# Inverse-spectra scratch by blocks of 128 rows, last transform in 128x32 tiles, and another order of operations in an H3 long convolution plus gated GLU with all gradients

## The chip, the cores and the metric

The kernel runs on one core of one Trainium2 chip. The metric is device microseconds of one execution, where less is better; the time of a kernel is the median of its runs. One further execution was recorded by the hardware profiler, and every line of a profile shown here comes from such a recording.

The engines go by these names: PE is TensorE (matmuls; PEld is the loading of their weights), DVE is VectorE, ACT is ScalarE, POOL is GpSimd, and SP is SyncE, which in this kernel issues every DMA (its queue is SPq). Data lies in a 2-dimensional on-chip memory of 128 partitions (here one array, `big`); matmul results land in PSUM (one array, `PP`).

## The reference, cut to what matters

The input is one sequence of S = 2048 rows and D = 512 channels in bf16. The function is a residual sum of a long convolution branch and a gated GLU branch over a normalised input; the kernel computes its value and the gradients of nine inputs for a given output gradient.

```python
xn = _layernorm(x)                       # x = A_q
# branch A: short shift convolution of k, times v, long convolution, times q
k_shift = sum over t of k_pad[:, t:t + S, :] * shift_k[:, ks - 1 - t]     # ks = 4
kv = k_shift * v
y = irfft(rfft(kv, 2 * S) * rfft(ssm_k, 2 * S))[:S] + kv * ssm_D
A = xn * y
# branch B, F = 1376
B = ((xn @ w_gate) * (xn @ w_up)) @ w_down
out = x + A + B
# and the vector-Jacobian product of out for A_q, A_k, A_v, shift_k, ssm_k, ssm_D, w_gate, w_up, w_down
```

The long convolution of length 4096 is done by matmuls with tables of sines and cosines, in two stages each way. Three spectra come back through the inverse transform: the convolution's value (in the code signal 0, `py[0]`), the gradient of kv (signal 1) and the gradient of ssm_k (signal 2). A row of the scratch that carries them between the two stages of the inverse therefore has 3 x 512 = 1536 elements, 3072 bytes.

## The kernel before

**Recording and order.** The body of the kernel runs no instruction itself. Every call goes through a small class `Eng`, which appends it to a list of operations; consecutive matmuls into the same PSUM slot, and the matmuls between `together()` and `apart()`, become one operation (a TensorE group). At the end `emit(PLAN)` unpacks a string: the order in which all operations are emitted, and the PSUM bank of every slot. The order of instructions on each engine, SyncE's DMA queue included, is the order of that list; nothing else decides it. Since all instructions are emitted by one line of `Eng`, every line of the profile says L173, and operations are told apart by tile names and shapes.

**Stages.** (1) The GLU's forward and data-gradient rows by strips j of F (0 to 5), with the strips' h, dg and du stored to a DRAM scratch `HD`; alongside it layernorm, and `dw_gen(j)`, the weight gradients of a strip, which end in stores of 1 MB and less to `ow`. (2) `a_gen`: first stage of the forward transforms, stored to the scratch `AX` in 16 stores of 768 KB. (3) `s_gen`, over i = 0 to 7: `s_B(i)` second stage forward, `s_pw` the pointwise products of spectra on VectorE, `s_Bi(i)` first stage inverse (L542). Each `s_Bi(i)` is three groups of 16 matmuls; ScalarE copies each result to one of two buffers `sp["C"][s]`, and four stores (L549) put them into the scratch `CX`, one of 384 KB for each s and g. (4) The rest goes by chunks n = 0 to 7 of 256 sequence rows:

- `c_load(n)` (L651 to L658) loads 1.5 MB of CX into `f["C"]`, of which there is only one: c_load(n+1) may start when the last transform of chunk n has read it. For n = 0 it is four loads, each to every fourth partition; three of them need no store of i = 7.
- `last_dft(n)` (L695 to L702) is the second stage of the inverse: 12 matmuls of 64 output rows, two side by side in the array.
- `c_dkv`, `c_y` and `c_o5` (L731 to L736) copy the three signals out of PSUM, multiply them by v, k_shift, xn and the output gradient, and store the results of v's and ssm_k's gradients (`o3`, `o5`; the first row of the latter also goes to `o6`, ssm_D's gradient).
- `c_dsk(n)` forms products for shift_k's gradient on VectorE and sums them over partitions by eight matmuls of 32 output rows (a P sum); `dk_pair` is k's gradient, on VectorE.
- `hd_load(n)` (L619) is a transposing DMA of the strips' rows from HD into one of two buffers; `y_o` and `y_x` are the block products with the weights (11 and 22 matmuls of 128x512 for each half chunk) that need it, and their results end in stores of `o0` and `o1`.

Each `hd_load` stands in SyncE's one queue with everything else. The order in that queue around the end of stage 3 is: weight-gradient store, the four stores of i = 7, hd_load(0), the last quarter of c_load(0), c_load(1). The buffers of the chunks lie partly over those of earlier stages in `big`: hd_load(1) overwrites the buffer from which the last weight-gradient store of strip 5 reads.

The scratch CX is declared with 8 chunks, each padded by 2048 elements (4 KB):

```python
CX = dram.tile([8, 512 * 3 * D + 2048], BF, name="CX")[:, 0:512 * 3 * D]
```

Of the kernel before, what the change touches and what calls it, by code (L numbers as in the profile page):

```python
# [10 lines left out]
BF = mybir.dt.bfloat16  # L11
# [6 lines left out]
S = 2048  # L18
D = 512
F = 1376  # L20
R = 16
# [6 lines left out]
NCH = 8  # L28
# [1 line left out]
RING = 28  # L30
RO = [0, 16, 24, 40, 56, 72]
EPS = 1e-5
PLAN = "c-lP|1FSC1uI&_au5H`4ZQHhO+qP}nwr$%s-*@hxyv)wFskUu4MPxt#hyu|e21J5%kRCEa2FM7RAPZ!LT#ya2LvF|ec_AM-U=UC+@DKzcAS8r>&=3Z~LO2Ky?H~f=fTR!;qC!Nd1;rp5#D=&K3(7+rC<^f)KBR>N;3Wklgk+E(DnLOf06C!$)P{;s2?|4TC;_FQG8BO-Pz|a=V`u{1p(*r$p3n?>!Dy%s?V&W(ff`T~2Ekw`3B92nG>7`o0s25c=nG?@E_8(c&;rInD;Nj!pe4+Q6>tPPL2GCL3!pO$fPpX`y1+u101e?WOocWu5hg(y=n7?F8nlI@Fdb&XZWscyU=eJD#jq5Xz$VxXTi_E+hD$IEX22d83M*j>#KjA+4A#IZh==iUD-4HiFdKHjcGw9Ca4jr{UGN!3z<$^ZA0ZK>hQyEx(!d<}1tVcK9DsfB1-`;TSO<q-J)D4(a14&aDL4(^AS5QlM3@-UVG=wC=`krL!{m4kZox&k4CmoG+<+_a9j?M{xCuYtCxpV3kOY#$ANT+j@gdxY6qpiI;RARAk03Rs!L;}cLSq<=h)*FbhQsg}0asxL%!rvVGiJf8$XE%pVP&j>*|93-z?_&1b7M8kgL$z!8Y&9r!@F<?&ca{Vh=hQMjj#qb#wOSlo8eGwjxDeyK8IE~3|~NNY=dpFCPv1n7zJx#ZES~iurAia_Baw>!zefm<={80#MQV4*Wx-{k8@!IguqC+AERLq=0}I!U^%L6LXV@cJ`TqYI09cn1MG;e;0?Tkw{QR(;%FR$8?XRQ#7Q_7$Kf;_j}ve@&cK=22@B#ZEQGVMFc!hixEZ(LHtd33u^V>B9@rCm;XGV`i?BBq#Xi^<n^8Y3hW&8>4#Yut5a;4#+>3{B3LeHII3E|{VqAhtaVt*6=va%kV{;meF>nPI#}ZhVVqt8oPbIMh)uuW4ga%SQiit;Y5DlgwG?b3xFgk_}s3p~*M%0joQxj@R?WqHu#8Oxq%V1e7hvo4EPN&m2gU;Y7Y)j{`0=A>ecm=OwREkE?DF(%)Yj_=F(G9$bx9~RJ!Mk`5@8bh}h_UGr#-X_M7@y!%e1`GpIljP`_zGX+8+?oJ@I8LOj~JigV1GJ~7jY(Cz*#h#E>bI+Lp$&je#S5O6~Ezk{DD957yiaS_!ohYh#Vy#CZU9sh!T^Mk*B#dg630ex<r?09$lfUv>S)u0BQt{={=mqeRu{g;Z({_L6n1XQZC9(A*dJa#9i2%_TYIMMR_PBC8Ok&f>Kf_3Qegf427j|l$Y{RcuGxaC@qzs{8W-kQE4heWvLuRpmda;GEjL+LP;qiWuyuei6T=)sze2-AQhs*RD_CBF)B`(s4``yEL4T6QZ>p-*{C`#q#Cq@I#M_4M2n~g^`!1}jTX~&8cAKKGxeqQG@3Th7FtVvXe_O!Z8V0q(l}a2YiK)7pdECOp3*aVPA_N@ZKO@Km-f>{+DVgX8kroTWwehD&>#9iyXhv~pqF%nR?uNuN>k_p-GlK|lUCAl`b)p)H~pkt^or2Ep;L69z`dr2befJ)825l4(Qyjv!nyG71iht`<lF~(M`!3grFH3CdY8dvbeY^OT1AiPBQ2o2beql+yE~NGWpP<uHkaL*%i%uJJ@W1gMRZ^3Gv#z~TrQW}#dYzVxcDxC3+0Bmgf5Xw?4rA2F0_l_hPudZxEtX{I(0!Vgp1;)xu`CN8|_B9Brd6o=3=>+Zn{h6lDiphyvySzx|uGoo8Tt73a+B7<i1fG`c5GvNTN_kS%wiLqC}F)u8OPbX1P!jT4uYku9{2Xs=F`}R>Db2m&#3X<J@EyULwn4m)b><t~B2*bSqpM*N<Ym{H~KL;0n4zuCOcOin?O1xGUj0yJ)h+EpiK7ESc+~N(_l3@g%w=kl3=!#g&*6Uy?{7NhpaWnWU7Gu8XVTYPwpklq>DZxU#OCOD(A+jg)s?T{qX=^>961ZI@QkNqVW{GD;>H<LbJ4u9xfW`nbNXzU$|*O9pA+a!P;K&^2-cTn=gM2D&D$sT<^yN(xCXxnzzjEK6M>$t`)LnQQL0xE5}!Yw4;<E7#hsbk(JX6q8jhi?nfVT{daw+Pl@Rjue$5QbI~fDJd?crHqu73Q}ImNkyqFm86PPm8`PHZFBcr2Ukz(N=LWWt#jL5K6jKdOHC;#1tg#3mHaZ;)t6e*KsHltx$hphhwhPk?4G!%?wNb;UbvU;m1`oe-5dATHI)zUqx<AOyD#pmYbftrGifZ1<eU5Mez?T^(<R~cZi8zsNjVuO=M<chQ*j4rFFRcq=_s9~t8|mj(p`E;FX<`0rJwYdzS2Tk%3w*&Y512*%jq~hXW$_+R7T2gx8G&ty)F}vlF@R&4U>H?GmntnZjU?U`p9s}%70vIX)A4{m4tNdWQ-hi17wg4lx#dl=E_8wB$FjO{|yW=$T@k6<Y3}lJXNO2CU@4IbLZU!w?Q_$i>@eNa+_qMjFZdmiW@Jvd7<oZ#dw0umwB>S^6(;AAWLPrtd=FRQkKaoSs`O3lG{V)0%dTz%#ztMQ)WnUKH*Nf&2rUUbJtx-zTs}VTkf_y=C())-YTVdo9vL|Zo3?DkvK9(;i#OK%kWw`>Q1@!vPMq3b&`)yisRi9jiYl6j>)k&Hpk((e8<IO=F)sh&d6ywFBfE|>~hQ9E}7?q_sCwk>kdjyJ|wlcI_Ky3d{}C50p2H7IRPi+f_zra$wj#&)%c2BmaB424#<8<#D(~=Je4P+Z0tFRLvTobAde&zm*voWS8DSOxh2=7Fc;xET#j$bL%A>aBn*e;id>!#yN&L+9Fe1POkPMOuE4M4r8MQ1+?B&|E3U$Kq#3`K(;S|gb2mQ2-T5rPl{eCY32sYe{x09-r~HsM{7(MJZ}}^~0;6YZMkRIHgL`sA?!~>i5BKE={6XH!8TU+{%L$q4zRG6_rHwcu*XMrRpYL;M4WnVT0YBh}99|!BIK9htc>p(I(I90FsrUE^*JIPi96{UiKpw>J`J;T1zx+wwyT}TXg(GStZOp3eIEs2rq#-n+e&A>tRnKupZqMhr6L;WPfx+l0zvaO^gkx(Qjjltv3wP$k`izt7J5Hi0HJK*W)S6aPXhuz?={1d}(@dIKGiVHrsTcSqU*zYULtpU={>bq(fyURkno~(G@nz1cSNJM_;#@j|XYwq*#@Bf^-{5STTW@l9{i%UsE_wA9&*8Z|kLPnf&7=8s0Wai5yqK5pQZAssbQu@a+gw<e^DrLHD|iHt<e&VSvuJ63!)3Ib7SZxrNy};lt)dmRvR2co`h{y~b*-tjw6@mKx>`>QX)!ITCAGMg(h@p~ckyl>&0}~hkK^$?fhY1F-pl*=J5S>Me1H$~WIn`Gcq$*}BYc#P@o_%EC;1ou;Awn{8|g~^%1v}SgZ<XOfuFFkHq}+Un%D4JZl=xk8-M2C{D<pnUtPy-w5_h^4ZM-tX?yLb{k4HM)Q!4{H}e1;sDreFZsCr)l{@Ku?W|q2t8UWGx<$8YH{GV&b%zetAv#od>Mp&i-L;4I)Lz<KxAAt~!Pj+|4%ZPnQb*}%y{%)kk6zOodRG_dZr!5`b&)RCCAw6X>2h76dv%|#)cv|jS8EGxsjan@#<vhAvXdX^9lfVx^^c;FvE1QtDz-+~>N-83>ouyWg|qM$(Sj_RMX>QYK_}`YJ*1QMp&r&FIz^A_F+Hv)^rTMJX*ykJ=qWv|Gj*2E)|)y<=juE?qi6M;p4SU{Q6t$S4QY`rifzzadQj)<C5>gdETt8;B9_!1Yg$WZMeVhwx0n{n!kAfD^A_9USTT!kX)Kkcws>|~^H>s#YghD%zR_fs+)`Ku%V?P_hSjjlmdzSie#>G7tftkn`j*x5S_vy@rL45Q*D_YtT3d5#VJ&Tl<+j>Z+&<`2eWraZyOpyXme?9vBdcSLt%>EcLKfQE+feIZ9qqYxvd&h}M%oMQV#6$<^|R`h)5==~t7J{BqP4MBHry&(SF2+EZIq3+F*er5*-QPZ8*HO(vJuwIs#-VeVFRtZ^|S#t-X_>Yn`{fLmrb&E_Dx^uAe(9RteUm8g;v)FTLPP9b8WM2v8{H*j@lYqWCv`UO|jXw!dBXMU1e|en4Pp!cG}L^S=(t-ZM*HT#kR{1+7jz+t8KUa(097jmf3NeZfk9w&9J_<*S!CzpESsyvk?BgU9gaTj~%l8mdNJWa+_vz?6A$ZeRjfb+6}vCm+h8)u#fi1Li;d&y}hx&_P{RL6?<rR?U6mUC-&4n+ZX$4SM8bIwr}>`ewy>--&$B7&WHCeEP{{df0+1d_RF4ILjOKc<iSVs*A0C}pUG$TFYT2T^RKPA&*Dq?tUjB+Z}-f6DF4nP`$RsmFX?|<6d%=R_kS#hPvT?yI6j(>@6{Ld(S0nR(wFwBd}?3Dm-V@PQlHG{^!a>RpWK)8<$VR8#uxVKd~Tn|SM+x*uCL@{_!K^auk5S(yuP6?<y-nzzP0b@hx%cDxbNgU`!2q#@8*m8n7)8d;A{GLzLrn#+xSL)gs<Wo`)a<BZ{lnFI=-!M>bv`1zK8GWtNZ%Cu5adx_)&heALGaRaelo2tY37!-{3d;O@6cA;s^QWzMik)^ZOQlfM4!c_?3R3Z|8ga_I`rz<2(3?eu1ClC;Ps>fgj>W`k8);-|FZ4ZN8tM>M!|KewN?v7y4;_k>BYT`yGC;pY2!sd47&x;t%-C{))fq&-!crx<BX7`-6U|-{)`mHU6fb;g|X8{(|rC=lWfKtv~FK_;voMzwM9tr~a3J=AZi){-uBAfBQfFuZJKEI__`z6aJ1r>G$~8{;q%H@A<cWx8LvI`S<>_zvxf-`+l!~;2-)!{*ez66gntmP?#VJ`rse?C*B2p@)E>BU%Uo=^%iv6pYb34H}8Xjg1-A7K2%WHpm0GyJ!zl-0~w%mLWY5%0NKz9Dm$kEZh-Af9S4>gA`UcYW>N@jf*4Q=@B_n0pl1Uh1&D!%7&u^1gSW<jF(;~l4blbh08@i?NfE)6#UQxj!+*5E6<`U-2b=(uzyKGJ2&|dv$Q-H@5f%(sLI43YhJg4#4^aagQTcaGj9q}K7L3_H0)hVj1aPImivl}ru=2m40)0O?Gz#`4m>!S{914yEg5iHB82d*Jh8!I2Kc#@{AQYUzz&G80$x-{44GqplU{?-yh|q-pfq?q~x&_=KHsfI6f+G#6I4}zIcm5xGy{0<"
KB = 1024


# [1 line left out]
def kernel(  # L38
# [30 lines left out]
    dram = ctx.enter_context(tc.tile_pool(name="dram", bufs=1, space=DRAM))  # L69
    HD = dram.tile([R, 640, 768], BF, name="HD")  # L70
    AX = dram.tile([128, 32, 3 * D], BF, name="AX")
    CX = dram.tile([8, 512 * 3 * D + 2048], BF, name="CX")[:, 0:512 * 3 * D]
    KS = dram.tile([128, 12, D], BF, name="KS")

    mem = ctx.enter_context(tc.tile_pool(name="mem", bufs=1))
# [130 lines left out]
    MM = nc.tensor.matmul  # L206
# [137 lines left out]
    n0 = [0]  # L344
# [187 lines left out]
    def s_Bi(i):  # L532
        for pr in range(3):
            pc = [v3(rF(), 2) for s in range(2)]
            together()
            for c in range(2):
                for q in range(4):
                    for s in range(2):
                        g, j = s_pair(s, q)
                        h = slice(32 * q, 32 * q + 32)  # L540
                        MM(pc[s][64 * j:64 * j + 64, g % 2, :], lhsT=et_tab(i)[h, s, c, :], rhs=sp["Y"][3 * s + pr][h, c, :], start=(c == 0), stop=(c == 1))
            apart()  # L542
            for s in range(2):
                ACOPY(sp["C"][s][:, :, pr, :], pc[s])
            yield
        for s in range(2):
            for g in range(2):
                st(CX.rearrange("n (g a e) -> g a n e", g=32, a=16)[4 * i + 2 * s + g], sp["C"][s][:, g].rearrange("p t d -> p (t d)"))

    def s_gen():  # L550
        for i in range(9):
# [97 lines left out]

    def c_load(n):  # L650
        c = f["C"].rearrange("p r e -> p (r e)")  # L651
        src = CX[n].rearrange("(t m e) -> m t e", t=4, m=32)
        if n:
            ld(c, src)
        else:
            for t in range(4):
                ld(c[t::4], src[:, t])

    def dkv_load(n):
        rs = slice(2 * n, 2 * n + 2)  # L660
# [33 lines left out]
    def last_dft(n):  # L694
        py = f["py"] = [v3(rF(), 2) for sig in range(3)]  # L695
        C = f["C"]
        together()
        for sig in (1, 0, 2):
            for rr in range(2):
                for h in range(2):  # L700
                    MM(py[sig][64 * h:64 * h + 64, rr, :], lhsT=W2, rhs=C[:, 2 * h + rr, sig * D:sig * D + D], start=True, stop=True)
        apart()  # L702

    def c_y(n):
# [252 lines left out]
def _tables():  # L957
# [5 lines left out]
    w1 = np.stack([np.cos(w1), -np.sin(w1)], -1).reshape(128, 128)  # L963
    k1, c = q // 2, q % 2
    w2 = 2 * np.pi * np.outer(2 * k1 + 1, np.arange(64)) / 256
    w2 = np.where((c == 0)[:, None], np.cos(w2), -np.sin(w2)).reshape(4, 32, 64).transpose(1, 0, 2).reshape(128, 64)
    j, c, r = q // 64, q // 32 % 2, q % 32
    m = (2 * np.arange(32)[None, :, None] + j[:, None, None]) + 128 * np.arange(32)
    a = 2 * np.pi * (2 * m + 1) * r[:, None, None] / 8192
# [7 lines left out]
    m = 2 * g + j + 128 * k2[:, None]  # L977
    a = (2 * np.pi * (2 * m + 1) / 8192)[:, :, None] * np.arange(32)
    et = np.stack([np.stack([np.cos(a), np.sin(a)], 2), np.stack([-np.sin(a), np.cos(a)], 2)], 2) / 2048
    et = et.reshape(128, 16, 2, 2, 2, 8, 2).transpose(0, 1, 2, 3, 4, 6, 5)  # L980
    tabs = np.concatenate([e.reshape(128, 8, 256), et.reshape(128, 8, 256)], 2)
    return np.concatenate([w1, w2, tabs.reshape(128, -1)], 1).astype(np.float32)

# [67 lines left out]
```

## Time and profile before

| | before |
|---|---|
| runs, us | 435.45, 432.09, 433.91 |
| median, us | 433.91 |
| span of the profiled execution, us | 429.5 |
| own time of the profiled execution | not listed; the median of the runs is 4.4 us above its span |
| PE busy | 419.6 us, 98% of the span |
| PEld busy | 204.1 us |
| DVE busy | 352.8 us, 82% |
| ACT busy | 267.3 us, 62% |
| DMA queue, share of 16 engines | 91.7% |
| bytes moved | 124.65 MB, 290 GB/s |
| granted TensorE clock | 1.00 |

The span runs from the first to the last instruction of the profiled execution. Busy time of an engine is the time in which one of its instructions runs; matmuls overlap in the array, so a busy PE need not be one at its peak pace. "DMA queue, share of 16 engines" is the time that the packets of the queue took, as a share of what 16 DMA engines have in the span. In lists of waits, a line has the waiting engine and tile, after the arrow what released it, then the total wait in us, the number of waits, and the longest. In timeline lines the columns are start and duration in us, engine, source line, instruction, output<-input, count. A line of the table by stages has the stretch, its length, then busy time and count of PE, PEld, DVE, ACT and POOL, the granted clock, the DMA share of 16 engines (packets counted side by side can bring it over 1), and GB/s. A line of DMA issues has output<-input, the number of issues, the size of each and the median time from issue to landing in us.

### The profile page before, as it was taken

To read this page: it belongs to the slowest core of one execution; us is meant where nothing else is said; L and a number is where in the kernel's file an instruction comes from. 1 tells how busy PE (TensorE), PEld (TensorE's weight loads), DVE (VectorE), ACT (ScalarE), POOL (GpSimd) and SP (SyncE) were. 2 spreads that over 40 slices of the span, in tenths; PEclk is the share of its full clock that TensorE was granted. 3 is DMA by queue.
4 is the path that set the end of the run, shared out by engine and by line. 5 is a ranking of instruction groups with operands and counts; after the bars stand their busy time and mean duration, and the time that the engine had idled before them with its cause. 6 is when DMAs were issued, how large, how long until landed. Compare 5 with 4: busy or idle time off the path is not lost.

```text
span 429.5 us, 8151 instructions
## 1 busy us (share of the span) xinstructions
PE 419.6 (98%) x3174; PEld 204.1 (48%) x3174; DVE 352.8 (82%) x684; ACT 267.3 (62%) x374; POOL 3.5 (1%) x9
## 2 busy tenths in 40 slices
PE   7999999999999999999999999889999999999996
PEld 4665455754454333544444344444444544444443
DVE  6799979998549989899999981044869989999996
ACT  2986879698554998988989963664244340313323
POOL 1000000000000000000000000000000000000000
PEclk9999999999999999999999999999999999999999
DMA  7997787959796979989989989999999999999933
GB/s 249 401 405 240 281 305 264 370 214 381 295 338 200 322 274 306 316 254 338 321 250 315 340 282 254 241 363 336 265 290 267 310 256 317 306 282 301 284 150 124
DMA packets 94878, 124.65 MB, mean 290 GB/s; under 512 B 53748, under 2 KB 63865, under 8 KB 93816
## 3 DMA queue, kind: packets, MB, share of 16 engines
q1 hardware_dynamic: 94840, 124.13, 91.7%
q8 instruction: 25, 0.41, 0.4%
q14 instruction: 13, 0.11, 0.1%
HBM read 57.10 MB, written 54.04 MB: 259 GB/s over the span
## 4 chain that ended last, share of the span: by engine, by line
PE 91%; DMA 6%; DVE 1%; SPq 1%; issue 1%; ACT 0%; ACTq 0%
PE PP L173 91%; DMA big<-CX 4%; DMA big<-in_goT_dram 1%; DVE big L173 1%; SPq L173 1%; ACT big L173 0%; ACTq L173 0%
## 5 line engine op out<-in xcount | busy, mean ns | idle before, releaser
L173 PE MATMUL PP<-big 128*128 128x512 bf16 (+9 forms) x3174 | 419.6, 347 | 5.8 <-issue 1.8
L173 PEld LDWEIGHTS <-big 128*128 128x128 bf16 (+5 forms) x3174 | 204.1, 98 | 221.0 <-issue 65.2
L173 DVE TENSOR_TENSOR big<-big 128x1024 bf16<-128x1024 bf16 (+4 forms) x465 | 269.3, 629 | 46.0 <-ACT big L173 42.6
L173 ACT CAST big<-PP 128x512 bf16<-128x512 f32 (+2 forms) x314 | 225.2, 780 | 90.0 <-PE PP L173 74.8
L173 ACT ACTIVATE big<-big 128x512 bf16<-128x512 f32 (+3 forms) x30 | 19.1, 645 | 40.8 <-DVE big L173 40.8
L173 DVE CAST big<-PP 128x512 bf16<-128x512 f32 (+1 forms) x37 | 32.3, 873 | 11.9 <-PE PP L173 10.0
L173 ACT COPY big<-PP 128x1024 bf16<-128x1024 bf16 x25 | 24.9, 1019 | 21.5 <-PE PP L173 21.5
L173 DVE SCALAR_TENSOR_TENSOR big<-big 128x1 f32<-128x1 f32 (+2 forms) x52 | 25.5, 498 | 0.6 <-ACT big L173 0.2
L173 DVE BATCH_NORM_STATS2 big<-big 128x6 f32<-128x512 bf16 x16 | 10.8, 679 | 2.7 <-DMA big<-in_x_dram 2.6
L173 DVE TENSOR_TENSOR big<-big,PP 128x512 bf16<-128x512 bf16 x14 | 9.5, 682 | 4.1 <-PE PP L173 4.0
L173 DVE SCALAR_TENSOR_TENSOR big<-big,PP 128x512 f32<-128x512 bf16 x14 | 9.5, 682 | 3.3 <-PE PP L173 3.3
L173 DVE TENSOR_SCALAR big<-big 128x1 f32<-128x1 f32 (+1 forms) x28 | 7.0, 259 | 0.2
L173 POOL MEMSET big<- 128x1536 bf16 (+2 forms) x3 | 2.8, 950 | 256.0 <-PE PP L173 252.7
L173 ACT ACTIVATE big<-PP 128x512 f32<-128x512 f32 x2 | 1.2, 598 | 5.5 <-PE PP L173 5.5
L173 DVE RECIPROCAL big<-big 128x2 f32<-128x2 f32 (+1 forms) x9 | 1.4, 155 | 3.7 <-ACT big L173 3.7
L173 DVE BATCH_NORM_AGGREGATE big<-big 128x2 f32<-128x6 f32 x16 | 2.8, 177 | 0.2
L173 ACT ACT_TABLE_LOAD x1 | 1.3, 1283 | 0.7 <-PEq L1039 0.7
L173 DVE DVE_READ_ACCUMULATOR big<-big 128x1 f32 x16 | 1.3, 81 | 0.0
L173 DVE DVE_READ_ACCUMULATOR big<-big,PP 128x1 f32 x14 | 1.1, 81 | 0.0
L173 DVE MEMSET big<- 128x1 f32 (+1 forms) x2 | 0.2, 112 | 0.8 <-PEq L1039 0.8
L173 DVE COPY big<-PP 128x1024 bf16<-128x1024 bf16 x1 | 0.7, 685 | 0.0
L173 ACT ACTIVATION_READ_ACCUMULATOR big<-PP 128x1 f32 x2 | 0.4, 194 | 0.0
(6 smaller groups left out, 0.9 us busy)
## 6 DMA issues: line engine op xcount, KB each, us to landing
HD<-big SPq DMA_DIRECT2D x32, 384.0 KB, 8.2
AX<-big SPq DMA_DIRECT2D x16, 768.0 KB, 5.1
big<-AX SPq DMA_DIRECT2D x16, 768.0 KB, 7.4
CX<-big SPq DMA_DIRECT2D x32, 384.0 KB, 4.5
out_dram<-big SPq DMA_DIRECT2D x44, 256.0 KB, 3.1
big<-CX SPq DMA_DIRECT2D x7, 1536.0 KB, 8.7
big<-in_v_dram SPq DMA_DIRECT2D x16, 256.0 KB, 6.2
big<-in_w_dram SPq DMA_DIRECT2D x4, 768.0 KB, 6.5
```

Of the source, the lines that this page charges most:

```text
L173: o.fns.append(lambda: f(*[fix(x) for x in a], **{kk: fix(x) for kk, x in k.items()}))
```

## The change

The scratch CX becomes 32 blocks of 128 rows, without padding. A step s of `s_Bi(i)` stores both of its g in one DMA of 768 KB to two neighbouring blocks, so 16 stores take the place of 32. `c_load(n)` reads from every block the 4 x 4 rows that belong to chunk n: 12,288 contiguous bytes for each partition, 96 KB apart. For n = 0 its four loads now go to 32 neighbouring partitions each. The last transform computes 32 output rows per matmul and sets four side by side in the array: 24 matmuls for a chunk instead of 12, with one half of the table W2 each. The tables `w2` and `et` on the host are permuted to suit. The string PLAN is another order with its own PSUM banks; it has 16 operations fewer.

Unpacked, the new order has 862 of 1019 TensorE groups, 586 of 654 VectorE operations, 238 of 371 ScalarE operations and 242 of 258 DMA issues at another place, counted on each engine's list after the dropped stores are taken out of the old one; a TensorE group moves by 45 places at most. SyncE's queue around the end of stage 3 reads: weight-gradient store, sk_load, the two stores of i = 7, the loads of ks and v, the last quarter of c_load(0), hd_load(0), weight-gradient store, c_load(1), y_load(0), the stores of chunk 0. The small store o6 stands behind c_load(2).

```diff
--- before.py
+++ after.py
@@ -30,7 +30,7 @@
 RING = 28
 RO = [0, 16, 24, 40, 56, 72]
 EPS = 1e-5
-PLAN = "..."
+PLAN = "..."
 KB = 1024
 
 
@@ -69,7 +69,7 @@
     dram = ctx.enter_context(tc.tile_pool(name="dram", bufs=1, space=DRAM))
     HD = dram.tile([R, 640, 768], BF, name="HD")
     AX = dram.tile([128, 32, 3 * D], BF, name="AX")
-    CX = dram.tile([8, 512 * 3 * D + 2048], BF, name="CX")[:, 0:512 * 3 * D]
+    CX = dram.tile([32, 128, 3 * D], BF, name="CX")
     KS = dram.tile([128, 12, D], BF, name="KS")
 
     mem = ctx.enter_context(tc.tile_pool(name="mem", bufs=1))
@@ -544,8 +544,8 @@
                 ACOPY(sp["C"][s][:, :, pr, :], pc[s])
             yield
         for s in range(2):
-            for g in range(2):
-                st(CX.rearrange("n (g a e) -> g a n e", g=32, a=16)[4 * i + 2 * s + g], sp["C"][s][:, g].rearrange("p t d -> p (t d)"))
+            b = 4 * i + 2 * s
+            st(CX[b:b + 2].rearrange("g p e -> p g e"), sp["C"][s].rearrange("p g t d -> p g (t d)"))
 
     def s_gen():
         for i in range(9):
@@ -649,12 +649,9 @@
 
     def c_load(n):
         c = f["C"].rearrange("p r e -> p (r e)")
-        src = CX[n].rearrange("(t m e) -> m t e", t=4, m=32)
-        if n:
-            ld(c, src)
-        else:
-            for t in range(4):
-                ld(c[t::4], src[:, t])
+        src = CX.rearrange("g (q n r) e -> n (g q) (r e)", q=4, n=NCH)[n]
+        for p in (slice(0, 128),) if n else (slice(32 * t, 32 * t + 32) for t in range(4)):
+            ld(c[p], src[p])
 
     def dkv_load(n):
         rs = slice(2 * n, 2 * n + 2)
@@ -697,8 +694,8 @@
         together()
         for sig in (1, 0, 2):
             for rr in range(2):
-                for h in range(2):
-                    MM(py[sig][64 * h:64 * h + 64, rr, :], lhsT=W2, rhs=C[:, 2 * h + rr, sig * D:sig * D + D], start=True, stop=True)
+                for h in range(4):
+                    MM(py[sig][32 * h:32 * h + 32, rr, :], lhsT=W2[:, h % 2 * 32:h % 2 * 32 + 32], rhs=C[:, h // 2 * 2 + rr, sig * D:sig * D + D], start=True, stop=True)
         apart()
 
     def c_y(n):
@@ -963,7 +960,7 @@
     w1 = np.stack([np.cos(w1), -np.sin(w1)], -1).reshape(128, 128)
     k1, c = q // 2, q % 2
     w2 = 2 * np.pi * np.outer(2 * k1 + 1, np.arange(64)) / 256
-    w2 = np.where((c == 0)[:, None], np.cos(w2), -np.sin(w2)).reshape(4, 32, 64).transpose(1, 0, 2).reshape(128, 64)
+    w2 = np.where((c == 0)[:, None], np.cos(w2), -np.sin(w2))
     j, c, r = q // 64, q // 32 % 2, q % 32
     m = (2 * np.arange(32)[None, :, None] + j[:, None, None]) + 128 * np.arange(32)
     a = 2 * np.pi * (2 * m + 1) * r[:, None, None] / 8192
@@ -977,7 +974,7 @@
     m = 2 * g + j + 128 * k2[:, None]
     a = (2 * np.pi * (2 * m + 1) / 8192)[:, :, None] * np.arange(32)
     et = np.stack([np.stack([np.cos(a), np.sin(a)], 2), np.stack([-np.sin(a), np.cos(a)], 2)], 2) / 2048
-    et = et.reshape(128, 16, 2, 2, 2, 8, 2).transpose(0, 1, 2, 3, 4, 6, 5)
+    et = et.reshape(128, 16, 2, 2, 2, 8, 2).transpose(0, 1, 2, 3, 5, 4, 6)
     tabs = np.concatenate([e.reshape(128, 8, 256), et.reshape(128, 8, 256)], 2)
     return np.concatenate([w1, w2, tabs.reshape(128, -1)], 1).astype(np.float32)
```

## Prediction before the run

> **What bounds the kernel now.** First the page: which engine is full, and how much of the span is free at all.
>
> ```profile
> span 429.5 us, 8151 instructions
> PE 419.6 (98%) x3174; PEld 204.1 (48%) x3174; DVE 352.8 (82%) x684; ACT 267.3 (62%) x374; POOL 3.5 (1%) x9
> q1 hardware_dynamic: 94840, 124.13, 91.7%
> ```
>
> TensorE is busy 98% of the span, and the DMA queue's packets fill 92% of 16 engines. So a gain can only come out of the few us in which TensorE stands, and late DMAs are what can make new ones. Second, what TensorE waits for:
>
> ```profile
> PE PP L173 <- issue: 1.8, 1, 1.8
> PE PP L173 <- DMA big<-CX: 1.6, 2, 1.2
> PE PP L173 <- DMA big<-in_goT_dram: 1.2, 1, 1.2
> PE PP L173 <- DVE big L173: 1.1, 1, 1.1
> ```
>
> A busy matmul outlasts its pace, so I take the starts of the matmuls: against the usual step of each shape, starts come 1.36 us late at 7.7 (first inputs), 1.93 at 276.1, 1.38 at 288.3 and 0.55 at 399.8. The last three stand before a last transform that waits for its piece of CX: 3.86 us, all within reach of this change. The other 8 us or so of lateness are tile-shape switches of 0.1 us each. Third, SyncE's timeline over the two large ones, since SyncE issues every DMA, in order:
>
> ```profile
> 260.17 3.23 SPq L173 DMA_DIRECT2D CX<-big  x4
> 263.50 10.77 SPq L173 DMA_TRANSPOSE big<-HD  x1
> 274.46 0.51 SPq L173 DMA_DIRECT2D big<-CX  x1
> ...
> 279.74 0.59 SPq L173 DMA_DIRECT2D big<-CX  x1
> ```
>
> The four last CX stores go out, then the transposing load hd_load(0) holds SyncE for 10.77 us, and only behind it comes the last quarter of c_load(0). It lands at 278.13, and the last transform of chunk 0 starts at 278.22. c_load(1) may overwrite the only C buffer after that (279.74), lands 10.1 us later, and chunk 1's transform starts at 289.90.
>
> **The change, part by part.** The own time of the profiled execution is not listed beside its span; the three runs have a median of 433.9, 4.4 above the span. I add up in the span and carry the 4.4 along.
>
> *1. Last transform in 128x32 tiles.* 96 matmuls become 192. What the trace shows of both shapes, by the weight loads of a P sum (128*32) followed by a last transform (128*64):
>
> ```profile
> 301.81 0.12 PEld L173 LDWEIGHTS <-big 128*32 128x32 bf16 x8 [0.42 <-issue]
> 302.36 1.00 PEld L173 LDWEIGHTS <-big 128*64 128x64 bf16 x12 [0.42 <-issue]
> 303.77 2.27 PEld L173 LDWEIGHTS <-big 128*128 128x128 bf16 x12 [0.41 <-issue]
> ```
>
> By matmul starts, four 128*32 begin within 10 ns and the next four 216 ns later; two 128*64 begin together and the next pair 213 ns later. Six pairs become six quads: 8 x 6 x 3 ns = +0.14 us. In both orders six of the eight last transforms stand right behind a P sum, in the new one of the same shape: the step of 309 ns between shapes becomes 216, 6 x 0.09 = -0.56. Sum -0.4. The extra 96 weight loads (94 ns each) I put at nothing: eight of them go out in 0.12 us here. But these eight share one weight tile and fill only two quads; six quads in a row with changing halves are not in the trace. If four loads ran one after another, a quad would take 376 instead of 216 ns: 48 x 0.16 = +7.7 us. Bounds -0.6 and +7.7; I take -0.4, the row with the same shape and engine.
>
> *2. Stores.* 16 of 768 KB replace 32 of 384 KB.
>
> ```profile
> AX<-big SPq DMA_DIRECT2D x16, 768.0 KB, 5.1
> CX<-big SPq DMA_DIRECT2D x32, 384.0 KB, 4.5
> big<-CX SPq DMA_DIRECT2D x7, 1536.0 KB, 8.7
> ```
>
> A CX store of half the size lands hardly earlier than an AX store; with nothing ahead of them the shortest are 3.3 and 3.7 us. The new store writes two runs of 384 KB, and AX stores are its nearest row. SyncE saves 16 issues of 0.59 us (9.4 us), hidden, since no TensorE wait before 270 ends on a store. It counts in part 3 alone.
>
> The new scratch drops the 4 KB of padding, and c_load now steps 96 KB from partition to partition. Row: AX stores step by the same 96 KB, and three of them landed in 3.7 to 3.9 us. The Trainium skill ("DMA: Bandwidth & Descriptors", section "Latency and other measured facts") speaks against leaving padding out: row pitches of large powers of two lost up to half the rate, 4 KB of padding restored it; its smallest pitch, 512 KiB, lost 3%. By its worst case a 1.5-MB load would take some 5 us more and the sum would be near 437; by the row it changes nothing. I go by the row, since 96 KB is the very step that it shows; the trace has no such loads.
>
> *3. From the last inverse transform to chunk 1.* The string in the diff is the list of operations in order, packed; unpacked beside the old one it gives the new places. Let zero be the start of the last inverse group (258.07 before). TensorE work after it, counted with the usual step of each shape: to chunk 0's transform 17.9 us before, 14.3 after; to chunk 1's 28.2 before, 26.7 after (the same place in TensorE's whole list).
>
> New chain: ScalarE's last copies end as before, so the two stores go out at +2.1 and +3.1. The first lands as the shortest AX store, +5.8; the second 768 KB later, at the 330 KB/us at which stores that queue up land here, +8.2. The last quarter of c_load(0) is now ahead of hd_load(0): out at +8.3, 3.8 us (the old pieces took 3.7 to 5.1), TensorE ready at +12.1, needed at +14.3: the 1.93 us is gone. Slowest rows (8.8 for a store): +15.7, 1.4 late.
>
> hd_load(0) moves back by the load's place, to +8.8. Its time on SyncE was 7.73 to 11.05; 7.7 to 8.4 where little was in flight, 10 to 11 behind a whole c_load or fresh stores. I take 8.6, because only 384 KB stand before it: free at +17.4. Then a weight-gradient store (0.5) and c_load(1) at +17.9; chunk 0's transform is done at +15.7, so it doesn't wait. Median landing 8.7: +26.6, against +26.7. With the 10.1 of before it is 1.3 late, with the 10.77 of hd_load too 3.5. I take 0.6. Together 3.31 becomes 0.6: -2.7 (from -3.3 to +1.6).
>
> Behind c_load(1) now stand y_load(0), the stores of dv(0) and o5(0) and the loads of v and ks: VectorE waits for these, but it is busy only 8.04 of the 24 us here:
>
> ```profile
> 276.00:300.00 24.00, 21.02 (x133) 10.20 (x131) 8.04 (x11) 11.84 (x14) 0.00 (x0) 1.00 0.97 338
> 350.00:392.00 42.00, 42.00 (x217) 18.42 (x216) 40.97 (x85) 9.73 (x12) 0.00 (x0) 1.00 1.13 283
> 392.00:419.60 27.60, 27.21 (x143) 12.43 (x142) 27.21 (x61) 8.59 (x11) 0.00 (x0) 1.00 0.80 234
> ```
>
> *4. New waits behind it.* The small store o6 is moved behind c_load(2). ScalarE's o5 copy of chunk 1 overwrites what o6 reads, so it waits: c_load(2) goes out when chunk 1's transform ends (+1.4 from its start), lands 8.7 later, copy 1.0: bank free 11.1 us after chunk 1's transform, needed 13.5 after it (its third signal comes last). Cost 0, at most 1.5. hd_load(1) waits for the last weight-gradient store, whose buffer it overwrites: gradients end with +26.7, copies 1.5, store out +28.5, landed by the median +34; hd_load(1) lands 11.2 to 13.2 later, +45 to +47; the first block product of chunk 1 needs it at +46.7. I take 0.5, between 0 and 2.5.
>
> *5. Start and end.* In the new order goT's first piece moves up by two issues, but the big first weight piece keeps its 2.3 MB ahead of it and landed at 12.0, and TensorE needs it after the same work: -0.3 (between -1.4, the whole wait, and +0.6). c_load(7) has two issues fewer ahead of it (1.1 us): its 0.55 goes, -0.5. The tail from TensorE's last matmul to the last store keeps its operations: 0, give or take 1.
>
> *6. The rest of the order.* 862 of 1019 TensorE groups change place, by 45 at most. Before, no other wait exceeds 0.3 us. From 350 on VectorE is busy 98%, so what comes late there is not caught up. Between 0 and +4 (all lateness of before outside the switches, once more); I take +1.3.
>
> Sum: -0.4 - 2.7 + 0 + 0.5 - 0.3 - 0.5 + 1.3 = -2.1. Span 427.4, time 431.8.
>
> **The rivals.** *The transposing load holds c_load(1)* (slower). Decides from a hold of about 8.7 us on: every us more is a us at chunk 1, and then at hd_load(1). At the old 10.77 and 10.1: 3.5 there instead of 3.3, part 4 at its upper ends 4.0, part 6 at 1.8, less 1.2 of part 1, c_load(7) and the start: +0.2 + 4.0 + 1.8 - 1.2 = +4.8, 438.7. For it: six of eight holds were above 8.6, and 92% DMA use. Against it: those stood behind more bytes. Chance 0.21.
>
> *Weight loads don't keep up*: -2.1 + 0.4 + 7.7 = +6.0, 439.9; chance 0.04, against eight loads in 0.12 us.
>
> *Everything fits*: part 3 at -3.3, part 5 at -1.9, part 1 at -0.6, parts 4 and 6 at 0: -5.8, 428.1. For it: the four places are all that TensorE loses in one piece. Against it: a list with so many moves. Chance 0.22.
>
> *No gain because the place isn't on the path*: excluded, as every us there is TensorE's. The forecast holds with 0.53.
>
> **How the numbers follow.** About 1% (4.3 us) is what a measurement of this kernel can tell from no change; the runs of before differ by 3.4. The forecast lies within: 0.53. Faster 0.22, slower 0.21 + 0.04. The range runs from the best case, 428.0, to just below the weight-load rival, 439.5; 430 to 434.5 is the likeliest case's own.
>
> **What would show it.** Right: matmul 128*32 x256, CX stores x16; chunk 0's transform without a wait and less than 1 us before chunk 1's; TensorE idle of some 3 us in place of 5.8. Wrong: hd_load(0) above 9.5 us, or CX waits that are longer than before (parts 3 and 4); many waits of TensorE on DVE or ACT after 300 (part 6); quads more than 230 ns apart (part 1).

## The result, and the profile after

| | before | after |
|---|---|---|
| median of six runs each, us | 434.28 (432.09 to 435.67) | 429.86 (428.42 to 430.52) |
| ratio after to before | | 0.989, 95% interval 0.9862 to 0.9918 |
| span of the profiled execution, us | 429.5 | 427.9 |

Six runs of the new kernel lasted 1.8 us longer than their spans, and later runs of the old one show the same 1.8. The profiled execution of before (429.5) therefore took some 431.3 us, less than any of the six runs. Ratios leave out runs that lie more than 1.5% above the fastest of their kernel; medians are of all runs. What an ordinary run of before loses beyond it is one of the questions below.

The page after, the lines of engine totals and of the DMA queue:

```profile
span 427.9 us, 8313 instructions
PE 418.4 (98%) x3270; PEld 203.4 (48%) x3270; DVE 352.5 (82%) x684; ACT 268.3 (63%) x374; POOL 3.4 (1%) x9
q1 hardware_dynamic: 94584, 124.13, 89.7%
```

The 96 extra matmuls are there and add nothing to PE's busy time; the same bytes take 2 points less of the DMA engines. TensorE's list of waits after (waiting engine and tile, releaser: total, times, longest):

```profile
PE PP L173 <- DVE big L173: 2.6, 3, 1.1
PE PP L173 <- DMA big<-AX: 1.3, 1, 1.3
PE PP L173 <- DMA big<-in_goT_dram: 0.5, 1, 0.5
```

The waits for CX are gone; one for AX and two more for VectorE have come. By starts of matmuls, against the usual step of each shape: nothing at chunk 0, 0.29 us at chunk 1, nothing at chunk 7 (before: 1.93, 1.38, 0.55); new are 1.68 us at 139.4 (a load from AX), 1.12 at 346.9 (VectorE, itself late by 0.83 for a load of x), 0.35 at 307.3 and 0.33 at 332.8. SyncE's timeline after (start, duration) at the end of the inverse:

```profile
262.24 1.29 SPq L173 DMA_DIRECT2D CX<-big  x2
...
269.46 0.32 SPq L173 DMA_DIRECT2D big<-CX  x1
269.88 8.25 SPq L173 DMA_TRANSPOSE big<-HD  x1
...
278.85 0.37 SPq L173 DMA_DIRECT2D big<-CX  x1
```

The last quarter of c_load(0) goes out as the second store lands (269.45), hd_load(0) behind it holds SyncE for 8.25 us, and c_load(1) follows behind one store. The weight loads of a last transform, and the DMA issues (count, size, median us to landing):

```profile
300.33 1.42 PEld L173 LDWEIGHTS <-big 128*32 128x32 bf16 x32 [0.42 <-issue]
```
```profile
CX<-big SPq DMA_DIRECT2D x16, 768.0 KB, 4.9
big<-CX SPq DMA_DIRECT2D x7, 1536.0 KB, 7.9
```

Eight weight loads of a P sum and 24 of the transform go out in one run in 1.42 us, and the quads begin 215 to 227 ns apart, nearly all of them 216: they keep their pace. A store of twice the size lands 4.9 us after issue, where half of it took 4.5.

### The profile page after: what moved, and what is told of

The parts are those of the page before. It is cut to its first block, busy times and chain, and to the rows that moved or that the text cites. A ratio compares the mean times of both kernels' runs of the same rounds, so it can differ in the third digit from the quotient of the medians.

```text
span 427.9 us, 8313 instructions
## 1 busy us (share of the span) xinstructions
PE 418.4 (98%) x3270; PEld 203.4 (48%) x3270; DVE 352.5 (82%) x684; ACT 268.3 (63%) x374; POOL 3.4 (1%) x9
## 4 chain that ended last, share of the span: by engine, by line
PE 76%; DMA 12%; DVE 7%; SPq 3%; issue 1%; ACT 1%; DVEq 0%
PE PP L173 76%; DVE big L173 7%; DMA out_dram<-big 3%; DMA big<-HD 3%; SPq L173 3%; DMA big<-in_x_dram 2%; DMA big<-AX 2%; DMA big<-in_w_dram 2%; ACT big L173 1%; DVEq L173 0%
## 5 line engine op out<-in xcount | busy, mean ns | idle before, releaser
L173 PE MATMUL PP<-big 128*128 128x512 bf16 (+8 forms) x3270 | 418.4, 347 | 5.3 <-DVE big L173 2.6
L173 PEld LDWEIGHTS <-big 128*128 128x128 bf16 (+4 forms) x3270 | 203.4, 97 | 219.8 <-issue 62.3
L173 ACT CAST big<-PP 128x1024 bf16<-128x1024 f32 (+2 forms) x314 | 225.8, 779 | 86.3 <-PE PP L173 64.1
L173 DVE CAST big<-PP 128x512 bf16<-128x512 f32 (+1 forms) x37 | 32.2, 874 | 16.8 <-PE PP L173 12.1
L173 DVE TENSOR_TENSOR big<-big,PP 128x512 bf16<-128x512 bf16 x14 | 9.5, 682 | 10.2 <-PE PP L173 10.1
```

What stands on the lines that cost most here:

```text
L173: o.fns.append(lambda: f(*[fix(x) for x in a], **{kk: fix(x) for kk, x in k.items()}))
```

## The experiments

The first theory is that of the prediction: the gain is the order at one place, the quarter of c_load(0) ahead of hd_load(0). The rivals are that the stores themselves make the difference, or the tiles. Each kernel was compared with the kernel before on the same chip; three chips were used, and the kernel before has medians of 432.87, 433.76 and 432.32 us on them.

**Taking the change apart.** Four kernels: the old one again; the old one with quads; new scratch and tiles in the old order; old scratch and tiles in the new order.

> The kernel before, unchanged, to see what an ordinary run of it loses. Its profiled run had a span of 429.5 us; the runs of the changed kernel last 1.8 us longer than their spans, so the six runs of the kernel before (median 434.3) should have spans of about 432.5. Theory 'one place': the missing 3 us are more waiting of TensorE for DMAs at the last transforms of chunks 0, 1 and 7 (3.9 us in the profile so far, 5 to 7 here). Rival 'late everywhere': several waits of 0.5 us and more at other places. Both expect 434.3 +- 1.

> The kernel before with nothing but the last transform in 128x32 tiles. Theory 'one place': -0.4 us (the trace of the changed kernel has the same step between starts, less a switch of shape), so a ratio of 0.997 to 1.001. Rival 'tiles': the whole gain of 4.4 us, ratio 0.990.

```diff
-                for h in range(2):
-                    MM(py[sig][64 * h:64 * h + 64, rr, :], lhsT=W2, ...)
+                for h in range(4):
+                    MM(py[sig][32 * h:32 * h + 32, rr, :], lhsT=W2[:, h % 2 * 32:h % 2 * 32 + 32], ...)
```

> The changed kernel in the old order: 16 stores of 768 KB at the place of the first of each old pair, unpadded blocks, 128x32 tiles, old PSUM banks. Theory 'one place': hd_load(0) still stands ahead of the last quarter of c_load(0), so the waits before chunks 0 and 1 stay at 3 us or more and the ratio is 0.996 to 1.002. Rival 'lighter queue': fewer and longer stores relieve the DMA queue (89.7% instead of 91.7% of 16 engines) wherever TensorE waits for one, and most of the gain is here, ratio 0.990 to 0.993.

```diff
 (the changed kernel)
-PLAN = the new order
+PLAN = the old order and its banks, each pair of stores replaced by one at the place of the first
```

> The kernel before in the new order: 32 stores of 384 KB into the padded chunks, the second of each pair right behind the first, last transform in 128x64 tiles. Theory 'one place': the waits before chunks 0 and 1 are gone (under 1 us together), 0.4 us of tile switches come back, ratio 0.989 to 0.993. Rival 'lighter queue': ratio 0.997 to 1.003.

```diff
 (the kernel before)
-PLAN = the old order
+PLAN = the new order and its banks, the second store of each pair right behind the first
```

| kernel | scratch | order | median, us | ratio to before | interval |
|---|---|---|---|---|---|
| b_again | old | old | 432.44 | 0.999 | 0.9955 to 1.0025 |
| b_quads | old, quads | old | 432.54 | 0.9982 | 0.9954 to 1.0011 |
| c_oldorder | new | old | 429.87 | 0.9932 | 0.9899 to 0.9965 |
| d_neworder | old | new | 434.09 | 1.0003 | 0.9972 to 1.0034 |

The theory fails. The new scratch with its tiles, hd_load(0) still ahead of the quarter, is 0.7% faster; the new order alone gains nothing. Tiles alone: between -0.5% and +0.1%, which agrees with the -0.7 us that the steps show (below) and cannot confirm it. In TensorE's longest waits in c_oldorder the line for CX, which was chunk 1's, is gone, and the longest of the `issue` line, chunk 0's, has fallen from 1.8 to 0.8:

```profile
PE PP L173 <- issue: 2.3, 10, 0.8
PE PP L173 <- DMA big<-HD: 1.4, 2, 1.0
PE PP L173 <- DVE big L173: 1.1, 1, 1.1
```

Two traces say more. The new order without the new stores does take away the waits before chunks 0 and 1 (both below 0.2 us). It pays for that earlier, in stage 3. TensorE's timeline of d_neworder, and ScalarE's waits:

```profile
164.68 1.55 PE L173 MATMUL PP<-big 128*128 128x512 bf16 x19 [1.06 <-ACT big L173]
```
```profile
183.72 0.62 PE L173 MATMUL PP<-big 64*32 64x512 bf16 x15 [1.59 <-DMA big<-AX]
```
```profile
ACT big L173 <- DMA CX<-big: 1.5, 1, 1.5
```

ScalarE's copy waits 1.5 us for a CX store to free its buffer, and TensorE 1.06 for ScalarE; then a load of AX, issued at 171.39 behind four stores instead of at 169.42 behind two, costs 1.59. So the order's gain is given back in part behind the old stores: once behind their landing, once behind their issues. Its other waits (1.06 us for a table at 239, 0.79 for HD at 311) were not followed up.

b_again's median, 432.44, lies below the 434.3 +- 1 that both theories expected. Its profiled execution is the second longest of its twelve (435.71 us, span 433.9). Its waits, and its table by stages around chunk 1 (after the stretch and its length: PE, PEld, DVE, ACT, POOL, clock, DMA share, GB/s):

```profile
PE PP L173 <- issue: 3.0, 8, 1.9
PE PP L173 <- DMA big<-CX: 2.5, 2, 2.2
PE PP L173 <- DMA big<-in_goT_dram: 2.4, 1, 2.4
```
```profile
289.00:291.00 2.00, 1.08 (x6) 0.29 (x3) 0.00 (x0) 1.70 (x4) 0.00 (x0) 1.00 1.03 341
291.00:293.00 2.00, 0.75 (x6) 0.41 (x8) 0.00 (x0) 0.00 (x0) 0.00 (x0) 0.89 0.87 267
293.00:295.00 2.00, 2.00 (x11) 0.53 (x8) 0.00 (x0) 0.15 (x1) 0.00 (x0) 0.50 1.00 396
295.00:297.00 2.00, 1.95 (x7) 0.80 (x7) 0.00 (x0) 2.00 (x3) 0.00 (x0) 0.76 0.55 149
```

TensorE stands 2.17 us before chunk 1, and then the granted clock is 0.50 for 3.4 us (0.89, 0.50 and 0.76 as means over 2 us are 0.44, 2 and 0.96 us at half). Half the work of 3.4 us is 1.7 us lost, behind a wait that is itself only 1 us longer than in the first profile. The list of waits doesn't show it, since TensorE is busy meanwhile.

**What in the new scratch does it?** Candidates: the time that SyncE needs to issue (four stores ahead of hd_load(0) take 3.2 us, two of the new ones 1.3), the count, or the transfer itself.

> Old order and the new unpadded blocks, but 32 stores of 384 KB again, one whole block of 128 rows each; last transform in 128x32 tiles. It differs from c_oldorder by the number of stores alone. Theory 'SyncE's issue time': what pays is the time that SyncE spends on the stores of i = 7 ahead of hd_load(0), 3.3 us for four in the kernel before, 1.4 us for two of the new ones. Four of the new form at 0.4 to 0.5 us should take 1.7 to 2 us: nearer to c_oldorder, ratio 0.993 to 0.997, hd_load(0) out 0.4 to 0.7 us later after the last inverse group than in c_oldorder. Rival 'count': each store costs SyncE the same, four take 3 us again and the ratio is 0.997 to 1.001. Rival 'faster transfer': the stores' landing sets c_load(0), ratio 0.993 and no change of SyncE's part.

```diff
-            st(CX[b:b + 2].rearrange("g p e -> p g e"), sp["C"][s].rearrange("p g t d -> p g (t d)"))
+            for g in range(2):
+                st(CX[b + g], sp["C"][s][:, g].rearrange("p t d -> p (t d)"))
```

> c_oldorder with four tiny loads (32 bytes each, into a spare tile that nothing reads) put ahead of hd_load(0). Theory 'SyncE's issue time': four issues of about 0.4 us send hd_load(0) and with it the last quarter of c_load(0) off 1.6 us later, the waits before chunks 0 and 1 grow by 1.6 to 2.9 us, ratio 0.997 to 1.000. Rival 'transfer': bytes and packets are those of c_oldorder, ratio 0.993.

```diff
+    for q in range(4):
+        ld(spare[0:1, 16 * q:16 * q + 16], D_d[0:1, 16 * q:16 * q + 16])
     emit(PLAN)    # the four stand ahead of hd_load(0)
```

g_split: 0.9932 (0.9895 to 0.997), the same as c_oldorder. h_delay: 0.9921 (0.989 to 0.9952), nothing lost, against the theory of issue time, which expected 0.997 or more. SyncE's timelines of b_again, c_oldorder, g_split and h_delay, in this order:

```profile
261.40 3.24 SPq L173 DMA_DIRECT2D CX<-big  x4
264.74 10.91 SPq L173 DMA_TRANSPOSE big<-HD  x1
275.84 0.51 SPq L173 DMA_DIRECT2D big<-CX  x1
```
```profile
259.15 1.30 SPq L173 DMA_DIRECT2D CX<-big  x2
260.54 11.00 SPq L173 DMA_TRANSPOSE big<-HD  x1
271.66 0.50 SPq L173 DMA_DIRECT2D big<-CX  x1
```
```profile
260.96 2.30 SPq L173 DMA_DIRECT2D CX<-big  x4
263.37 9.52 SPq L173 DMA_TRANSPOSE big<-HD  x1
273.07 0.42 SPq L173 DMA_DIRECT2D big<-CX  x1
```
```profile
259.65 1.29 SPq L173 DMA_DIRECT2D CX<-big  x2
261.00 3.14 SPq L173 DMA_DIRECT2D big<-in_D_dram  x4
264.23 6.70 SPq L173 DMA_TRANSPOSE big<-HD  x1
271.04 0.51 SPq L173 DMA_DIRECT2D big<-CX  x1
```

The four tiny loads cost SyncE 3.1 us, and hd_load(0) holds it 4.3 us less. Against the start of the last inverse group of each trace, in us:

| kernel | last store lands | hd_load(0) out | hold | SyncE free | quarter lands | idle before chunks 0 and 1 |
|---|---|---|---|---|---|---|
| before | 12.05 | 5.43 | 10.77 | 16.20 | 20.06 | 1.77, 1.21 |
| b_again | 12.20 | 5.44 | 10.92 | 16.36 | 20.22 | 1.93, 2.17 |
| b_quads | 12.52 | 6.09 | 10.40 | 16.49 | 20.38 | 1.43, 1.48 |
| c_oldorder | 9.03 | 3.49 | 11.00 | 14.49 | 19.11 | 0.83, below 0.2 |
| g_split | 10.03 | 4.51 | 9.52 | 14.03 | 18.81 | 0.52, 0.37 |
| h_delay | 7.64 | 6.68 | 6.70 | 13.38 | 17.88 | below 0.2, 0.61 (ScalarE) |

In all six the transposing load lets SyncE go 4.0 to 5.7 us after the last store ahead of it has landed, no matter when it was issued. So time that SyncE spends on issues behind the stores is lost in that hold, and a landing that is 2.0 to 4.4 us sooner than in before frees SyncE 1.7 to 2.8 us sooner.

The new stores do land sooner, g_split's at equal count and bytes. The first 512 packets of 3072 bytes from the first CX store of i = 3, 6 and 7 on, counted from the traces (in ns), and the time from that first issue to the last landing (in us):

```
kernel       mean          nine tenths below  landing, i = 3, 7  neighbouring partitions write
before       145 152 174   239 247 294        7.5, 10.0          1.5 MB + 4 KB apart
b_quads      154 157 179   251 265 289        7.2, 9.8           1.5 MB + 4 KB apart
d_neworder   153 156 163   258 253 267        7.2, 7.5           1.5 MB + 4 KB apart
q_nopad      157 151 172   260 239 292        7.7, 8.8           1.5 MB apart
g_split      126 127 152   138 129 222        6.1, 7.9           next to each other
c_oldorder   126 126 171   133 131 258        5.4, 6.9           next to each other
h_delay      127 126 127   133 131 131        not listed, 5.5    next to each other
after        127 150 150   135 229 229        5.4, 7.2           next to each other
```

At i = 3 the contrast is clean. Half of the CX packets take 121 to 126 ns in every kernel; of the old stores' 16 to 22% take over 200 at i = 3, of the new ones' at most 1%. At i = 7, the place that counts here, the packets alone don't tell the kernels apart: c_oldorder's, with hd_load(0) out beside them, are as slow as those of before, and h_delay's, where it goes out 3.2 us later, are not. In the changed kernel a fifth of the packets take over 200 ns at i = 6 and 7, though no transposing load is out then; why is open. Part of the sooner landing is issue time after all: the last store of i = 7 goes out 2.1 us after the first in before, 1.4 in g_split, 0.9 in c_oldorder, which is 0.7 and 1.2 us of the 2.0 and 3.0. h_delay doesn't speak against this part, since its loads stand behind the stores.

Chunk 1's wait hangs on c_load(1) too, which goes out only after chunk 0's transform. It took 10.1 to 11.1 us to land in before, b_again and b_quads, 8.8 in c_oldorder and 9.3 in g_split. The new scratch changes this load as well (neighbouring partitions read 96 KB apart instead of 384 KB), and no kernel has the new stores with the old loads. q_nopad, with the old loads, has 9.3 us and 0.35 us of idle time at chunk 1, so the old load is not always slow; the shares of stores and loads at chunk 1 stay open.

**The padding** (q_nopad is the kernel before without it):

> The kernel before with the 4 KB of padding between the chunks of CX taken out, nothing else. Theory 'address step': the packets of its CX stores are slow (mean 148 to 174 ns, nine tenths below 240 to 290, where blocks of consecutive rows have 125 to 134 ns) because neighbouring partitions write 1.5 MB apart, with or without 4 KB; without padding they stay as slow or get slower: mean 150 or more, last landing 7.5 us or more after the first issue, ratio 0.998 to 1.015. Rival 'padding': the 4 KB are what misaligns them, packets at 125 to 134 ns and a ratio of 0.993 to 0.997.

```diff
-    CX = dram.tile([8, 512 * 3 * D + 2048], BF, name="CX")[:, 0:512 * 3 * D]
+    CX = dram.tile([8, 512 * 3 * D], BF, name="CX")
```

Ratio 1.0021 (0.999 to 1.0053), the packets as slow as before. An effect of the 4 KB isn't shown in either direction. What is slow is the pattern of the old store, rows of one store 1.5 MB apart; AX stores, 96 KB apart, have means of 121 to 140 ns in before, so not every large step is slow. Which property of the 1.5-MB step makes it slow was not tried.

**The order at the one place.** The swap alone, in both directions:

> The changed kernel with hd_load(0) ahead of the last quarter of c_load(0), as in the old order, all else of the new order kept. Theory 'the order at this place': hd_load(0) goes out at about 266.2 and holds SyncE for 8.3 to 11 us, the quarter lands 4.3 us later at 279 to 281.6, TensorE wants it at 274.8, so 4.2 to 6.8 us are lost: ratio 0.999 to 1.005 to the kernel before, 1.010 to 1.016 to the changed one. Rival 'the rest absorbs it': 0.989 to 0.992 to the kernel before.

> The kernel before with that one swap: the last quarter of c_load(0) ahead of hd_load(0), nothing else. Working from its trace: the quarter goes out at 270.2 when the last store has landed, lands at 274 to 275, so the 1.9 us before chunk 0 are gone; hd_load(0) goes from 270.7 to about 279.7, five issues still stand between it and c_load(1), which goes out at 282.4 and lands at 290.4 to 292.4, 3.8 to 5.8 us after TensorE wants it, where it lost 3.3 us in all before: ratio 1.001 to 1.006. Rival 'the swap is the gain of the new order': ratio 0.990 to 0.995.

```diff
 e_swap, the changed kernel:   v, c_load(0) quarter, hd_load(0)   ->   v, hd_load(0), c_load(0) quarter
 f_swap, the kernel before:    hd_load(0), c_load(0) quarter      ->   c_load(0) quarter, hd_load(0)
```

e_swap: 1.0105 (1.0067 to 1.0143), above its range; TensorE stands 5.12 us before chunk 0, as worked out, and then works 5.5 us at a granted clock of 0.50, which costs 2.8 us more. f_swap: 1.0062 (1.0024 to 1.0099), as expected: chunk 0 has no wait, chunk 1 has 4.18. The order that the change chose is right for its own queue, and the swap without the other moves makes the old kernel slower.

**Is it the clock?** f_swap, with work put into its wait:

> f_swap with 14 extra matmuls of 128x512 ahead of the last transform of chunk 1, into its own PSUM bank, where the transform then overwrites them (3.0 us of work that serves nothing, inside a wait of 4.2 us). Theory 'clock': in f_swap the clock granted to TensorE falls to 0.50 for 3 to 4 us from the long wait on, which costs some 2.5 us on top of the wait; with the wait shortened to about 1.2 us the clock stays at 1.00 and the ratio to the kernel before falls from 1.006 to about 1.000. Rival 'the wait alone': the extra matmuls change nothing that TensorE waits for, ratio 1.005 to 1.007.

```diff
         together()
+        for i in range(14 if n == 1 else 0):
+            MM(py[1][:, 0, :], lhsT=W1, rhs=go[:, i, :], start=True, stop=True)
         for sig in (1, 0, 2):
```

The table by stages of f_swap, then of f_warm:

```profile
289.00:291.00 2.00, 0.00 (x0) 0.00 (x0) 0.00 (x0) 0.00 (x0) 0.00 (x0) 0.76 1.01 354
293.00:295.00 2.00, 2.00 (x10) 0.48 (x7) 0.00 (x0) 0.58 (x1) 0.00 (x0) 0.50 0.94 374
295.00:297.00 2.00, 2.00 (x6) 0.74 (x5) 0.00 (x0) 2.00 (x3) 0.00 (x0) 0.54 0.66 193
```
```profile
293.00:295.00 2.00, 2.00 (x11) 0.88 (x9) 0.00 (x0) 2.00 (x3) 0.00 (x0) 1.00 1.14 347
295.00:297.00 2.00, 2.00 (x17) 1.15 (x16) 0.69 (x1) 1.64 (x2) 0.00 (x0) 1.00 0.99 360
```

With 14 matmuls that serve nothing the clock stays at 1.00, 17 matmuls run from 295 to 297 instead of 6, and the span falls from 434.0 to 430.9. The ratio is 1.004 (1.0008 to 1.0072), between the two expectations; its interval and that of f_swap overlap, so the time alone does not settle it, the clock rows do. Of f_swap's nine runs eight had a mean clock of 0.9965 or less, of f_warm's twelve two.

**A version from it.** VectorE's wait for y_load(3) is the one that the changed kernel repeats.

> The changed kernel with y_load(3) right behind hd_load(3), ahead of the small copies and c_load(4). In its trace VectorE waits 0.83 us for that load at 344 and TensorE 1.07 us for VectorE behind it. The load goes out 1.5 us earlier, both waits should vanish: 0.5 to 1.1 us less than a_again, ratio to the kernel before 0.987 to 0.988 where a_again has 0.989. Rival 'it only moves': the 0.4 us that c_load(4) goes out later come back at chunk 4, ratio as a_again.

> The changed kernel once more, on the chip of the other runs of this call: 429 to 431 us, ratio 0.987 to 0.992, and, since its waits are all below 1.7 us, no run with a lowered clock: highest and lowest run less than 3 us apart, where the runs of the kernel before spread over 7.

```diff
 SyncE, the changed kernel:   hd_load(3), copies, c_load(4), y_load(3)   ->   hd_load(3), y_load(3), copies, c_load(4)
```

a_again: 429.59 us, 0.9943 (0.9911 to 0.9974), a smaller gain than the 0.987 to 0.992 expected. a_better: 427.83 us, 0.9923 (0.9895 to 0.9952), the lowest median of all though not the 0.987 to 0.988 expected, and the idle time of 1.24 us that a_again has at 345 is below 0.2; but 0.82 us stand at 331 instead, TensorE ends 0.34 us earlier, and the intervals overlap: a gain over the changed kernel isn't shown. a_again's runs spread over 5.2 us, more than expected; one of twelve had the lowered clock.

## Why the prediction was right, and where not

431.8 was predicted (428.0 to 439.5) and 429.86 measured: a small gain, as forecast, but for the most part by another route than the one given. The span came out as added up (427.4, measured 427.9); since the old order has most of the gain too, that is luck as far as the reason goes.

- **The base.** "I carry the 4.4 along" failed. Runs lie 1.8 us above their own spans, and the 2.6 beyond it were losses that the profiled execution did not have. Of 90 later runs of the kernel before, 35 had a mean clock of 0.9965 or less and a median of 434.3, the other 55 a median of 432.2; the clock of the six runs of the first comparison is not on record. With 1.8 the predicted span of 427.4 gives 429.2.
- **Part 1, tiles:** -0.4 predicted. A P sum and the transform behind it now take 1.84 us from their first start to that of the next shape, 1.96 before; a transform alone takes 1.41 and took 1.42: -0.7 over eight chunks. The weight loads keep up.
- **Part 2, stores:** this is the step that failed. "It counts in part 3 alone" put the stores at nothing and their gain on the order. The AX row was right for the new store at i = 3 (127 ns a packet), less so at i = 6 and 7 (150). But I did not carry through that the old store's packets were slow, 145 to 174 ns in before, nor that fewer issues let the last store go out sooner, and so what the new scratch is worth in the old order too: 0.7%, tiles included.
- **The rule on padding** that was weighed against the change (the Trainium skill, "DMA: Bandwidth & Descriptors", section "Latency and other measured facts") has no counterpart here: q_nopad shows no effect of 4 KB at a 1.5-MB step, and the unpadded loads landed in 7.9 us against 8.7. Neither 1.5 MB nor 96 KB is a power of two, so the rule itself was not put to the test.
- **Part 3, the chain**, in us from the last inverse group, predicted and measured: last store landed 8.2 and 8.98; quarter out 8.3 and 9.00, landed 12.1 and 13.34, needed 14.3 and 14.35; hd_load(0) out 8.8 and 9.42, hold 8.6 and 8.25; c_load(1) out 17.9 and 18.39, landed 26.6 and 27.05; lateness at chunk 1 0.6 and 0.29. The chain was right, its attribution not: c_oldorder gets most of it without the swap.
- **Part 4:** 0.5 predicted, 0.35 measured at 307.3, where hd_load(1) lands; o6 costs nothing at chunk 2.
- **Part 5:** the start gained nothing (-0.3 predicted): TensorE's idle time from 2 to 12 us was 1.20 and is 0.49 + 0.51 + 0.25; c_load(7)'s 0.55 is gone. In the trace the late starts given as 7.7 and 399.8 are those at 9.5 and 401.2. **Part 6:** +1.3 predicted; the last matmul ends 1.73 earlier than before, so the remainder is +2.2, with the waits at 139.4 (absent in a_again) and 346.9 (there again, 1.24 us idle) as its largest parts.
- **The rivals:** the hold was 8.25 us, below the 8.7 from which that rival decides. Missing was the one that came nearest: the new scratch as the cause in any order, and the clock as the price of a wait.

Where the gain lies, then: runs without the lowered clock have medians of 432.2 before and 428.7 to 429.3 for c_oldorder, g_split, h_delay and a_again, some 3 us, of which the idle time before chunks 0 and 1 (2.9 to 4.1 us in before, b_again and b_quads, but 2.0 in q_nopad; 0.6 to 0.9 with the new scratch in the old order) makes 1 to 3.5. Beyond these 3 us, fewer runs have the lowered clock, 7 of 48 in these four against 35 of 90. That the order adds to it is not shown: 0.989 and 0.9943 with it, 0.9921 to 0.9932 without.

## What to carry to other kernels

Where a store's rows go is part of its price: before an order is searched, look how long the packets of a store take beside those of another store of the same packet size, since a slow store delays everything behind it in its queue. An issue that seems to hold an engine may only be waiting for what is ahead of it; delay it on purpose, and see whether its end moves. Before a gain is worked out from one profile, compare that execution's time with the runs: a wait near a threshold makes two kinds of runs, and the profile shows one.

## What the runs showed of the hardware

**The clock can fall after a wait of little more than 2 us.** Idle times of TensorE of 2.17 us (b_again) and 2.48 (b_quads) were followed by 3.4 us at a granted clock of 0.50. With those of 4.18 (f_swap) and 5.12 (e_swap) it lasted 6.8 us, twice as long, and began 1.5 and 1.3 us before the wait ended. Idle times of 1.93 (b_again, before chunk 0), 2.09 (q_nopad) and 2.40 (b_again, at 8 us) were not, so length alone does not decide. TensorE's timeline of q_nopad, and its table by stages behind the wait, with the clock at 1.00:

```profile
129.57 0.63 PE L173 MATMUL PP<-big 64*32 64x512 bf16 x16 [2.09 <-DMA big<-AX]
```
```profile
129.60:131.00 1.40, 1.40 (x20) 0.52 (x20) 0.65 (x1) 0.74 (x1) 0.00 (x0) 1.00 0.67 255
```

The Trainium skill ("TensorE: Matmul & The Clock Gate") has a free-running window of 3413 ns (section "Part 1: The HAM clock gate") and, as a rule, no idle gaps over about 3 us (section "Why this matters for your kernels"). The lengths of 3.4 and 6.8 us agree with the window; the rule is too wide for these runs, where 2.17 us were enough.

**The transposing load's hold on SyncE** is not a length of its own: before chunk 0 it was 6.70 to 11.00 us, and where it was issued before the last store had landed (the six rows of that table) it ended 4.0 to 5.7 us after the landing; q_nopad (5.3) and e_swap (5.4) agree. Only this one place was varied.
